# An attention, dense-MoE and routed-MoE kernel: register loads beside their branches, slot tables later, weight preparation and attention spread differently

## The chip, the cores and the metric

One core of one Trainium2 chip. The time is device microseconds of one execution; the kernel before took 888.47 us, the median of three runs (888.46 to 889.22). Lower is better. All durations below come from one profiled execution of the kernel before.

## The reference

Three stages, each feeding the next, on 4 batches of 576 tokens (2304 tokens, 512 features):

```python
# attention: 8 heads of 64; heads 0-3 with a local mask, heads 4-7 with a strided one (stride 32)
scores = where(mask, scale * q @ k.T, -1e9); attn = softmax(scores); x = attn @ v
# first MoE: LayerNorm and one dense feed-forward block for all tokens
xn = (x - mu) / sqrt(var + 1e-6) * g_ln
x = x + maximum(xn @ w_ch1, 0) @ w_ch2            # 512 -> 2048 -> 512
# second MoE: 8 experts, one for each token, 512 -> 1024 -> 512
e = argmax(logits)  where s == 0 or local_gate < 0.5, else the expert of the token before
out = softmax(logits)[e] * (maximum(x @ w1[e], 0) @ w2[e])
```

## The kernel before

TensorE (PE) computes every product with operands split into a high and a low part (three passes), so each weight has to be split before it is used. The program has one instruction stream for each engine; a planner written in Python puts the pieces of the stages into one another.

**First MoE with attention inside.** Tokens go in nine chunks `c` of 256. A step (c, f) is 24 matmuls: `mm1` (L628, matmuls at L635, result `ps_h`) for one block `f` of 16 of the hidden layer, ACT's ReLU (L637) and DVE's low part (L638), and `mm2` (L641, matmuls at L651, result `acc`). Chunks 0 and 1 run as pairs of interleaved steps, chunk 1 two steps behind (`LEAD`), because the weights are only arriving then; a step's number in that order is `t`. The dense weights come as 32 pieces `stg` by DMA, and each is split in a "weight turn": DVE L453, ACT L459 and L460 (`w_sign`), DVE L465, then the rounding to the high part at L479 (`w_split`, on ACT for all but the first four pieces) and POOL's subtraction L480 for the low part. `products` (L1050) decides before each step how many turns it issues: at least `need` (a turn for the weights that are read `WA` steps later), and otherwise `W_START + int(WR * t)`, with `W_START` 6 and `WR` 1.3 (L54, L1062, L1063). Attention of batch 0 stands ahead of the first chunk. That of batches 1, 2 and 3 is spread over spans of steps, `SPANS` (L51): the first from step 6 to step 24. It is made of units: transposes of q and k (L278), scores `ps_sc` (L317, L323), a softmax over DVE and ACT (`st`, `sm`: L335, L337, L350, L360 to L365), transposes of the probabilities (`ps_pt` L373, copied to `pt` at L381), and the product with v (`ps_o` L391, L409). The LayerNorm of chunk 1 (`ln_4`, variance matmuls at L571) stands between the first units.

**Routing and second MoE.** Tokens are listed by expert in tiles of 128. Four head tiles a0 to a3 of one expert, then the 14 sure tiles b0 to b13, whose expert is known only at run time, then leftovers in small slots; five slots s0, s1, s8, s9, s10 (`SURE`) always run, each behind the b-tile that `BEHIND` names (L67: 1, 3, 6, 9, 12). A tile is `e_mm1` (24 matmuls, L1396; the head tiles' at L1122), `h_prep` (transposes `ps_th` L1411, ACT L1412, DVE L1413 to `ht`), `e_mm2` (24 matmuls, L1424) and the weighted result `y` (L1427), scattered by POOL (L1428). For the head tiles the hidden layer's ReLU stands at L1126 (ACT) and its low part at L1127 (DVE). `x_prep` transposes the gathered tokens (`ps_tx` L878). A slot reads its weights unsplit from `raws`: L1358 (`s_mm1`) and L1384 (`s_mm2`).

Expert weights `raw` are split into `wx`, high at L778 (ACT) and low at L781 (DVE). Which tiles change the expert is known from a table `ti` only at run time, so each split and each load stands in a branch on a register: `flag` (L1306) loads one number of `ti` into a register of one engine, `resplit` (L1315) branches on it on ACT and on DVE, `next_load` (L1309) on SP, which issues the weight DMAs. In `run` (L1430) the first half of a tile's weights is split behind the product `e_mm1` of the tile before in the sequence, the second half behind `h_prep` of the tile itself, thus ahead of its `e_mm2`. In this run the expert changes at b4, b11 and b13. For slots, a table `ts` says if and for which expert (`used_s`, `load_small`). `small_places` (L1258) computes those tables, in a chain of small DVE instructions on one partition (`tb`, `vs`, `ts`; L1183 to L1188 and L1268 to L1279), then which tokens go to which slot (`chosen`: `ps_ve` L1227, `ps_ls` L1288 on PE). It is called just ahead of `e_mm2` of a2.

Of the kernel before, what the change touches and what calls it, by code (L numbers as in the profile page):

```python
# [18 lines left out]
ET = mybir.EngineType  # L19
# [5 lines left out]
NE, DF2 = 8, 1024  # L25
# [22 lines left out]
SMB, SM0, PT0, TL = 2, 4, 2, 1  # L48
WARM0, WARM, LB = 10, 5, 5
ORD = (((0, 1, 2), (0,)), ((3, 4, 5), (1,)), ((6, 7), (2,)))  # L50
SPANS = ((6, 24), (36, 54), (65, 86))  # L51

XB, LEAD = 5, 2
W_START, WR, WA, WI, W_DVE = 6, 1.3, 3, 5, 4  # L54
LN01, LN_AT, LN_W = (1, 1, 3, 1, 1, 4, 5, 9), (-7, -5, -4), (1, 2, 3, 4)
RT = ((0, 0, 1, 2, 3, 4, 6, 7, 8), (3, 4, 5, 6, 6, 7, 9, 10, 11))
RT_END = (0, 1, 2, 3, 4, 6, 8, 9, 10)
# [2 lines left out]
KA, NSURE = 4, 14  # L60
# [3 lines left out]
NLEAST = -(-(NT - NE * SMALL) // 128) - KA  # L64
NSM = 2 * NE
SURE = (0, 1, NE, NE + 1, NE + 2)
BEHIND = (1, 3, 6, 9, 12)  # L67
LAG1, LAG2 = 2, 4


# [1 line left out]
def attention_moe_moe(ctx: ExitStack, tc: tile.TileContext, q, k, v, g_ln, w_ch1, w_ch2, w_gate, w_local, w1, w2, out):  # L72
# [695 lines left out]
    def load_e(e, r, parts):  # L768

        if r < 2:  # L770
            src = w1[ds(e, 1)].rearrange("o d f -> (o d) f").rearrange("(i p) f -> p i f", p=128)[:, 2 * r:2 * r + 2]
        else:
            src = w2[ds(e, 1)].rearrange("o f d -> (o f) d").rearrange("(i p) o -> p i o", p=128)[:, 4 * (r - 2):4 * (r - 2) + 4]
        dst = parts[r]
        sp.dma_start(dst if r < 2 else dst.rearrange("p a (i o) -> p (a i) o", i=2), src)
# [479 lines left out]
    dve.tensor_copy(ti[:, 3, 0:NTILE], un)  # L1255


    def small_places():  # L1258

        vs = rt_p.tile([1, 2 * NSM], F32, tag="vs", name="vs").rearrange("p (a t) -> p a t", a=2)  # L1260
        dve.scalar_tensor_tensor(rem, cnt[:, 0, :], -128.0, cnt[:, 1, :], op0=ALU.mult, op1=ALU.add)
# [15 lines left out]
        dve.tensor_scalar(vs, vs, float(DM), None, op0=ALU.mult)  # L1277
        dve.tensor_tensor(over[:, 0:1], over[:, 0:1], over[:, 1:2], op=ALU.max)
        dve.tensor_tensor(ts[:, 2, 0:1], un[:, NSURE:NSURE + 1], over[:, 0:1], op=ALU.max)  # L1279
        sel, ix, er = chosen(vs, NSM, "_s")  # L1280
        for j in range(2):
            k = copies(NE * j)
            o = slice(NE * j, NE * j + NE)
# [19 lines left out]
    yp_ = [ps_acc.tile([128, 512], F32, tag=f"acc{i}", name=f"ps_y{i}") for i in range(2)]  # L1303
    turn = [0]

    def flag(i, n, engines):  # L1306
        return nc.values_load(ti[0:1, i, n:n + 1], engines=engines, min_val=0, max_val=NE - 1)

    def next_load(n, rs):  # L1309
        with tc.If(flag(1, n, [ET.SP]) > 0):  # L1310
            e = flag(2, n, [ET.SP])
            for r in rs:
                load_e(e, r, raw)

    def resplit(n, iis):  # L1315
        for eng, kinds, part in ((ET.Activation, ("InstActivation", "InstTensorCopy"), split_hi), (ET.DVE, ("InstTensorTensor",), split_lo)):
            last = next(i for i in reversed(nc.cur_bb.bb.instructions) if i.engine == eng and type(i).__name__ in kinds)
            v = flag(0, n, [eng])
            with tc.issue_after(last):
                with tc.If(v > 0):  # L1320
                    for j in iis:
                        part(j)
# [14 lines left out]
    pieces = {k: out.rearrange("t (h o) -> (t h) o", h=k) for k in (2, 4)}  # L1337

    def used_s(s, engines):
        return tc.If(nc.values_load(ts[0:1, 0, s[1]:s[1] + 1], engines=engines, min_val=0, max_val=1) > 0)  # L1340

    def set_of(i):
        return raw if i not in SURE and i % 2 == 0 else own

    def load_small(i):
        with used_s(("s", i), [ET.SP]):
            e = nc.values_load(ts[0:1, 1, i:i + 1], engines=[ET.SP], min_val=0, max_val=NE - 1)
            for r in range(4):
                load_e(e, r, set_of(i))

    def s_mm1(s):
        x, w, k = xs[s][0], set_of(s[1]), copies(s[1])
# [74 lines left out]
        act.activation(y, ps, AF.Copy, scale=pr)  # L1427
        pool.indirect_dma_start(out=out, out_offset=bass.IndirectOffsetOnAxis(ap=places(s)[1], axis=0), in_=y, in_offset=None, bounds_check=NT - 1, oob_is_err=False)  # L1428

    def run(seq, prev=None):  # L1430

        def weights(s, iis, rs):
            if s[0] == "b":
                resplit(s[1] + 1, iis)
                next_load(s[1] + 1, rs)

        for s in seq[:2]:
            if s not in xg:
                gather(s)
        if prev is None:  # L1440
            x_prep(seq[0])
            weights(seq[0], range(4), range(2))
        if len(seq) > 2:
            gather(seq[2])
        for i, s in enumerate(seq):
            e_mm1(s)
            if i + 1 < len(seq):
                x_prep(seq[i + 1])
                weights(seq[i + 1], range(4), range(2))
            p = seq[i - 1] if i else prev  # L1450
            if p:
                e_mm2(p)
                if p[0] == "s" and p[1] in SURE[:-1]:
                    load_small(SURE[SURE.index(p[1]) + 1])
            h_prep(s)
            weights(s, range(4, 8), range(2, 4))
            if i + 3 < len(seq):
                gather(seq[i + 3])
        e_mm2(seq[-1])

    for i in range(KA // 2):
        if i:
            e_mm1_two(i)
        for s in (("a", 2 * i + 2), ("a", 2 * i + 3)) if 2 * i + 2 < KA else (("b", 0),):
            if i:
                gather(s)
                x_prep(s)
        if 2 * i + 2 == KA:
            small_places()
            own += [new_blk([128, 2, 1024], F32, f"raws{r}") for r in range(4)]  # L1470
            load_small(0)
            resplit(1, range(4))
            next_load(1, range(2))
        for j in range(1 if 2 * i + 2 == KA else 2):
            e_mm2(("a", 2 * i + j))
    hp_ += [ps_m.tile([128, 512], F32, tag="m", name=f"ps_h2{i}") for i in range(2)]
    run([x for t in range(NSURE) for x in [("b", t)] + [("s", i) for i, b in zip(SURE, BEHIND) if b == t]], ("a", KA - 1))
    with tc.If(nc.values_load(ts[0:1, 2, 0:1], engines=mybir.ALL_ENGINES, min_val=0, max_val=1) > 0):  # L1478
        with tc.If(flag(3, NSURE, mybir.ALL_ENGINES) > 0):
            run([("b", t) for t in range(NSURE, NTILE)])  # L1480
# [38 lines left out]
```

## Time and profile before

| | |
|---|---|
| median of three runs | 888.47 us |
| the profiled execution's own time | 890.25 us |
| its span, first to last instruction | 888.5 us |
| mean granted TensorE clock | 0.985 |
| PE busy | 855.2 us (96%) |
| DVE, ACT, POOL busy | 469.9, 353.9, 148.5 us |

The profile shows one execution. An engine's busy time is the sum of its instructions; register loads, branches and DMA issues do not count in it. "Idle before" is the time for which an engine stood still ahead of an instruction, and the name behind the arrow is what ended that wait ("issue": nothing that the profile shows). PEclk is the TensorE clock that was granted, as a share of 2.4 GHz: 0.50 is 1.2 GHz.

### The profile page before, as it was taken

The page shows a single profiled execution, that of the slowest core. Times are in us where ns is not written, and L with a number is a line of the kernel's source. Part 1 is how long each engine was busy: PE and PEld are TensorE (multiplying, and loading weights), DVE is VectorE, ACT ScalarE, POOL GpSimd, SP SyncE. Part 2 cuts the span into 40 slices and gives each one's busy share as a digit, 9 for nine tenths or more (in the row PEclk, how much of TensorE's full clock was granted, in tenths as well). Part 3 has the DMA queues.
Part 4 walks back from the last instruction along what each step waited for, and adds up shares of the span by engine and source line. Part 5 has one row for each costly group of instructions (what it writes and reads, how often), then busy time and mean ns, then how long its engine had stood idle before and what let it go on. Part 6 is the DMA issues. An engine that isn't in the chain of part 4 may idle for free. (4 is left out here: it accounts for less than half of the span.)

```text
span 888.5 us, 18903 instructions
## 1 busy us (share of the span) xinstructions
PE 855.2 (96%) x7123; PEld 759.1 (85%) x7130; DVE 469.9 (53%) x1542; ACT 353.9 (40%) x857; POOL 148.5 (17%) x161
## 2 busy tenths in 40 slices
PE   9999898999999999999999999999989999999994
PEld 5678787899999999899999999999868777787873
DVE  4876676458656546666555554675731233211442
ACT  3687678542454233354211212332012244222543
POOL 2123233220120120120201212020221211210000
PEclk9999799999999999999999999999979999999998
DMA  9936245201212102210000000610446449440640
GB/s 182 261 112 207 55 130 144 56 8 52 65 41 45 49 13 61 49 26 18 23 1 25 1 25 2 214 49 26 166 157 225 149 147 391 153 144 27 242 165 16
DMA packets 96547, 87.17 MB, mean 98 GB/s; under 512 B 67378, under 2 KB 75574, under 8 KB 96440
## 3 DMA queue, kind: packets, MB, share of 16 engines
q1 hardware_dynamic: 89256, 69.61, 26.4%
q0 software_dynamic: 3552, 11.11, 3.8%
q10 hardware_dynamic: 3632, 5.09, 1.6%
q8 instruction: 59, 0.97, 0.4%
q14 instruction: 48, 0.39, 0.1%
HBM read 76.27 MB, written 9.97 MB: 97 GB/s over the span
## 5 line engine op out<-in xcount | busy, mean ns | idle before, releaser
L651 PE MATMUL acc<-h,w 128*128 128x256 f32 x1728 | 245.9, 290 | 2.4 <-DVE h L638 2.3
L635 PE MATMUL ps_h<-xc,w 128*128 128x256 f32 x1728 | 236.6, 286 | 0.1
L651 PEld LDWEIGHTS acc<-h,w 128*128 128x128 f32 x1728 | 218.8, 191 | 7.7 <-DVE h L638 3.6
L635 PEld LDWEIGHTS ps_h<-xc,w 128*128 128x128 f32 x1728 | 219.2, 192 | 2.1 <-DVE xc L619 0.5
L637 ACT ACTIVATE h<-ps_h 128x256 fp32r<-128x256 f32 x144 | 55.8, 388 | 221.4 <-PE ps_h L635 209.4
L638 DVE SCALAR_TENSOR_TENSOR h<-ps_h,h 128x256 fp32r<-128x256 f32 x144 | 60.5, 420 | 97.0 <-ACT h L637 96.7
L1396 PE MATMUL ps_h<-wx,xs 128*128 128x512 f32 x336 | 85.2, 409 | 0.0
L1424 PE MATMUL ps_y<-wx,ht 128*128 128x512 f32 x336 | 80.2, 394 | 2.0 <-ACT wx L778 1.7
L1396 PEld LDWEIGHTS ps_h<-wx,xs 128*128 128x128 f32 x336 | 64.3, 195 | 14.7
L1424 PEld LDWEIGHTS ps_y<-wx,ht 128*128 128x128 f32 x336 | 61.9, 188 | 15.2 <-ACT wx L778 2.3
L480 POOL TENSOR_TENSOR w<-stg,w 128x512 fp32r<-128x512 f32 x32 | 44.5, 1392 | 117.2 <-ACT w L479 75.6
L1427 ACT ACTIVATE y<-ps_y,pr 128x512 f32<-128x512 f32 x18 | 12.4, 687 | 84.5 <-PE ps_y L1424 56.7
L781 DVE TENSOR_TENSOR wx<-raw,wx 128x1024 fp32r<-128x1024 f32 x32 | 37.6, 1219 | 2.1 <-ACT wx L778 1.6
L1399 ACT ACTIVATE h<-ps_h 128x512 f32<-128x512 f32 x28 | 15.2, 595 | 58.8 <-PE ps_h L1396 58.8
L459 ACT ACTIVATE stg<-stg 128x512 f16<-128x512 f32 x27 | 37.1, 1375 | 0.2 <-DVE stg L453 0.2
L1413 DVE TENSOR_TENSOR ht<-ps_th,ht 128x512 fp32r<-128x512 f32 x28 | 18.1, 686 | 30.8 <-ACT ht L1412 27.4
L778 ACT CAST wx<-raw 128x1024 fp32r<-128x1024 f32 x32 | 31.9, 1055 | 6.4 <-PE acc L651 4.1
L892 DVE TENSOR_TENSOR xs<-ps_tx,xs 128x512 fp32r<-128x512 f32 x14 | 9.7, 691 | 46.3 <-ACTq L1320 35.3
L353 ACT ACTIVATE sm<-sm,st 128x54 f32<-128x54 f32 (+1 forms) x80 | 27.6, 347 | 13.3 <-DVE st L341 13.2
L1428 POOL DMA_INDIRECT out_dram<-y,idx x14 | 14.1, 1004 | 99.9 <-ACT y L1427 66.0
L894 DVE SCALAR_TENSOR_TENSOR pr<-io_e,e_rep,xg 128x8 f32<-128x8 f32 x14 | 3.1, 225 | 47.0 <-ACT y L1427 45.1
L1424 PE MATMUL ps_y<-wx,h2t 128*128 128x512 f32 x96 | 25.9, 414 | 1.5 <-DVE h2t L1127 1.3
(393 smaller groups left out, 1207.0 us busy)
## 6 DMA issues: line engine op xcount, KB each, us to landing
raws<-in_moe_w_dram SPq DMA_DIRECT2D x20, 1024.0 KB
stg<-in_moe_w_ch_dram SPq DMA_DIRECT2D x32, 512.0 KB
raw<-in_moe_w_dram SPq DMA_DIRECT2D x16, 1024.0 KB
xrows<-row ACTq DMA_DIRECT2D x9, 520.0 KB
qnat<-in_q_dram SPq DMA_DIRECT2D x48, 72.0 KB
knat<-in_k_dram SPq DMA_DIRECT2D x48, 72.0 KB
v<-in_v_dram SPq DMA_DIRECT2D x24, 72.0 KB
v<-in_v_dram SPq DMA_DIRECT2D x72, 18.0 KB
```

Of the source, the lines that this page charges most:

```text
L353: act.activation(sm[0:m, i, :], (ps if mode else sm)[0:m, i, :], AF.Exp, bias=st[0:m, 0, i:i + 1], scale=-1.0, **({} if mode else dict(acc ...
L459: keep(act.activation(t.bitcast(F16)[..., 1], f32(t[..., 1]), AF.Copy, scale=2.0 ** -112))
L480: keep(pool.tensor_tensor(w[:, 1], r, f32(w[:, 0]), op=ALU.subtract))
L635: pe.matmul(ps, w[:, a, d, o:o + 128], xcs[c][:, b_, d, :], start=(i == 0), stop=(i == 11))
L637: act.activation(h[:, 0, :], ps, AF.Relu)
L638: dve.scalar_tensor_tensor(h[:, 1, :], ps, 0.0, f32(h[:, 0, :]), op0=ALU.max, op1=ALU.subtract)
L651: pe.matmul(accs[c][d // 2][:, d % 2, :], w[:, a, f % 2, d * 128:(d + 1) * 128], h[:, b_, :], start=(f == 0 and (a, b_) == (0, 0) and d % ...
L778: act.copy(wx[i][:, 0, :], raw[i // 2][:, i % 2, :])
L781: dve.tensor_tensor(wx[i][:, 1, :], raw[i // 2][:, i % 2, :], f32(wx[i][:, 0, :]), op=ALU.subtract)
L1396: pe.matmul(hp_[fg], s_[:, a, d, :], wx[d][:, b_, 512 * fg:512 * fg + 512], start=(i == 0), stop=(i == 11))
L1413: dve.tensor_tensor(s_[1][:, 4 * g:4 * g + 4, :], ps, f32(s_[0][:, 4 * g:4 * g + 4, :]), op=ALU.subtract)
L1424: pe.matmul(ps, s_[a][:, f, :], wx[4 + f // 2][:, b_, 512 * (f % 2):512 * (f % 2) + 512], start=(i == 0), stop=(i == 23))
```

## The change

- The weight turns of the first MoE are issued at 1.0 a step instead of 1.3, and the first attention span goes from steps 6 to 24 to steps 8 to 26.
- `small_places` becomes two functions. The tables (`small_tables`) are computed in `run`, behind `e_mm1` of b0 and ahead of `e_mm2` of a3, and the places (`chosen` and what follows) behind `h_prep` of b0.
- A register's number is loaded once for each engine and kept (`loaded`), and its load stands just ahead of the branch that uses it, behind the last instruction that was put on that engine (`tc.issue_after`; `behind`).
- Slot s0 stands behind b2 instead of b1, and s1 behind b4 instead of b3.

```diff
--- before.py
+++ after.py
@@ -48,10 +48,10 @@
 SMB, SM0, PT0, TL = 2, 4, 2, 1
 WARM0, WARM, LB = 10, 5, 5
 ORD = (((0, 1, 2), (0,)), ((3, 4, 5), (1,)), ((6, 7), (2,)))
-SPANS = ((6, 24), (36, 54), (65, 86))
+SPANS = ((8, 26), (36, 54), (65, 86))
 
 XB, LEAD = 5, 2
-W_START, WR, WA, WI, W_DVE = 6, 1.3, 3, 5, 4
+W_START, WR, WA, WI, W_DVE = 6, 1.0, 3, 5, 4
 LN01, LN_AT, LN_W = (1, 1, 3, 1, 1, 4, 5, 9), (-7, -5, -4), (1, 2, 3, 4)
 RT = ((0, 0, 1, 2, 3, 4, 6, 7, 8), (3, 4, 5, 6, 6, 7, 9, 10, 11))
 RT_END = (0, 1, 2, 3, 4, 6, 8, 9, 10)
@@ -64,7 +64,7 @@
 NLEAST = -(-(NT - NE * SMALL) // 128) - KA
 NSM = 2 * NE
 SURE = (0, 1, NE, NE + 1, NE + 2)
-BEHIND = (1, 3, 6, 9, 12)
+BEHIND = (2, 4, 6, 9, 12)
 LAG1, LAG2 = 2, 4
 
 
@@ -1255,7 +1255,9 @@
     dve.tensor_copy(ti[:, 3, 0:NTILE], un)
 
 
-    def small_places():
+    tabs = []
+
+    def small_tables():
 
         vs = rt_p.tile([1, 2 * NSM], F32, tag="vs", name="vs").rearrange("p (a t) -> p a t", a=2)
         dve.scalar_tensor_tensor(rem, cnt[:, 0, :], -128.0, cnt[:, 1, :], op0=ALU.mult, op1=ALU.add)
@@ -1277,7 +1279,11 @@
         dve.tensor_scalar(vs, vs, float(DM), None, op0=ALU.mult)
         dve.tensor_tensor(over[:, 0:1], over[:, 0:1], over[:, 1:2], op=ALU.max)
         dve.tensor_tensor(ts[:, 2, 0:1], un[:, NSURE:NSURE + 1], over[:, 0:1], op=ALU.max)
-        sel, ix, er = chosen(vs, NSM, "_s")
+        tabs.append(vs)
+
+    def small_places():
+
+        sel, ix, er = chosen(tabs[0], NSM, "_s")
         for j in range(2):
             k = copies(NE * j)
             o = slice(NE * j, NE * j + NE)
@@ -1303,20 +1309,34 @@
     yp_ = [ps_acc.tile([128, 512], F32, tag=f"acc{i}", name=f"ps_y{i}") for i in range(2)]
     turn = [0]
 
+    regs = {}
+
+    def loaded(t, i, n, engines, top):
+        key = id(t), i, n, str(engines)
+        if key not in regs:
+            regs[key] = nc.values_load(t[0:1, i, n:n + 1], engines=engines, min_val=0, max_val=top)
+        return regs[key]
+
     def flag(i, n, engines):
-        return nc.values_load(ti[0:1, i, n:n + 1], engines=engines, min_val=0, max_val=NE - 1)
+        return loaded(ti, i, n, engines, NE - 1)
+
+    def behind(eng):
+
+        last = next((i for i in reversed(nc.cur_bb.bb.instructions) if i.engine == eng), None)
+        return tc.issue_after(last) if last is not None else ExitStack()
 
     def next_load(n, rs):
-        with tc.If(flag(1, n, [ET.SP]) > 0):
-            e = flag(2, n, [ET.SP])
-            for r in rs:
-                load_e(e, r, raw)
+        with behind(ET.SP):
+            v, e = flag(1, n, [ET.SP]), flag(2, n, [ET.SP])
+            with tc.If(v > 0):
+                for r in rs:
+                    load_e(e, r, raw)
 
     def resplit(n, iis):
         for eng, kinds, part in ((ET.Activation, ("InstActivation", "InstTensorCopy"), split_hi), (ET.DVE, ("InstTensorTensor",), split_lo)):
             last = next(i for i in reversed(nc.cur_bb.bb.instructions) if i.engine == eng and type(i).__name__ in kinds)
-            v = flag(0, n, [eng])
             with tc.issue_after(last):
+                v = flag(0, n, [eng])
                 with tc.If(v > 0):
                     for j in iis:
                         part(j)
@@ -1337,16 +1357,17 @@
     pieces = {k: out.rearrange("t (h o) -> (t h) o", h=k) for k in (2, 4)}
 
     def used_s(s, engines):
-        return tc.If(nc.values_load(ts[0:1, 0, s[1]:s[1] + 1], engines=engines, min_val=0, max_val=1) > 0)
+        return tc.If(loaded(ts, 0, s[1], engines, 1) > 0)
 
     def set_of(i):
         return raw if i not in SURE and i % 2 == 0 else own
 
     def load_small(i):
-        with used_s(("s", i), [ET.SP]):
-            e = nc.values_load(ts[0:1, 1, i:i + 1], engines=[ET.SP], min_val=0, max_val=NE - 1)
-            for r in range(4):
-                load_e(e, r, set_of(i))
+        with behind(ET.SP):
+            e = loaded(ts, 1, i, [ET.SP], NE - 1)
+            with used_s(("s", i), [ET.SP]):
+                for r in range(4):
+                    load_e(e, r, set_of(i))
 
     def s_mm1(s):
         x, w, k = xs[s][0], set_of(s[1]), copies(s[1])
@@ -1427,7 +1448,7 @@
         act.activation(y, ps, AF.Copy, scale=pr)
         pool.indirect_dma_start(out=out, out_offset=bass.IndirectOffsetOnAxis(ap=places(s)[1], axis=0), in_=y, in_offset=None, bounds_check=NT - 1, oob_is_err=False)
 
-    def run(seq, prev=None):
+    def run(seq, prev=None, tables=None, lists=None):
 
         def weights(s, iis, rs):
             if s[0] == "b":
@@ -1447,6 +1468,9 @@
             if i + 1 < len(seq):
                 x_prep(seq[i + 1])
                 weights(seq[i + 1], range(4), range(2))
+            if i == 0 and tables:
+                tables()
+                load_small(0)
             p = seq[i - 1] if i else prev
             if p:
                 e_mm2(p)
@@ -1454,6 +1478,8 @@
                     load_small(SURE[SURE.index(p[1]) + 1])
             h_prep(s)
             weights(s, range(4, 8), range(2, 4))
+            if i == 0 and lists:
+                lists()
             if i + 3 < len(seq):
                 gather(seq[i + 3])
         e_mm2(seq[-1])
@@ -1466,15 +1492,13 @@
                 gather(s)
                 x_prep(s)
         if 2 * i + 2 == KA:
-            small_places()
             own += [new_blk([128, 2, 1024], F32, f"raws{r}") for r in range(4)]
-            load_small(0)
             resplit(1, range(4))
             next_load(1, range(2))
         for j in range(1 if 2 * i + 2 == KA else 2):
             e_mm2(("a", 2 * i + j))
     hp_ += [ps_m.tile([128, 512], F32, tag="m", name=f"ps_h2{i}") for i in range(2)]
-    run([x for t in range(NSURE) for x in [("b", t)] + [("s", i) for i, b in zip(SURE, BEHIND) if b == t]], ("a", KA - 1))
+    run([x for t in range(NSURE) for x in [("b", t)] + [("s", i) for i, b in zip(SURE, BEHIND) if b == t]], ("a", KA - 1), small_tables, small_places)
     with tc.If(nc.values_load(ts[0:1, 2, 0:1], engines=mybir.ALL_ENGINES, min_val=0, max_val=1) > 0):
         with tc.If(flag(3, NSURE, mybir.ALL_ENGINES) > 0):
             run([("b", t) for t in range(NSURE, NTILE)])
```

The order of the instructions moves in places that the diff doesn't show. Numbers in tile names are buffers; lines of the changed kernel are 21 to 24 higher in this stretch. On **PE where attention of batch 1 begins** (`ps_tr` transposes, `ps_sc` scores, `ps_pt` transposes of the probabilities; `w_1_879` and so on are the weights of one turn):

```order
 L651 MATMUL acc_933<-h,w_1_879 128x256 x2
 L635 MATMUL ps_h<-xc,w_2_953 128x256 x12
-L278 MATMUL ps_tr<-iw,knat 128x96 x5
 L651 MATMUL acc_1074<-h,w_0_677 128x256 x6
 L651 MATMUL acc_1075<-h,w_0_677 128x256 x6
+L635 MATMUL ps_h<-xc,w_1_854 128x256 x12
+L651 MATMUL acc_932<-h,w_2_1040 128x256 x4
+L651 MATMUL acc_933<-h,w_2_1040 128x256 x4
+L651 MATMUL acc_932<-h,w_2_1040 128x256 x2
+L651 MATMUL acc_933<-h,w_2_1040 128x256 x2
+L635 MATMUL ps_h<-xc,w_2_953 128x256 x12
+L278 MATMUL ps_tr<-iw,knat 128x96 x5
```

The last transposes stand two steps later, and so does all that follows them. The variance matmuls L571, which stood behind the first `ps_pt` before, now stand ahead of it, behind the first scores.

On **ACT between the head tiles and b0** (`ti` is the routing table in SBUF, the `ISA` rows belong to the loads). Before, around the ReLU of the fourth head tile:

```order
L1307 TENSOR_LOAD ti
L1307 ISA x2
L1126 ACTIVATE h2t<-ps_h2t 128x512
L891 CAST xs<-ps_tx 128x512
L1320 COMPARE_AND_BRANCH
L778 CAST wx_7650<-raw_7649 128x1024
```

After the change:

```order
L1126 ACTIVATE h2t<-ps_h2t 128x512 x4
L891 CAST xs<-ps_tx 128x512
L1317 TENSOR_LOAD ti
L1340 COMPARE_AND_BRANCH
L778 CAST wx_7650<-raw_7649 128x1024
```

Before, five or six such loads stood between each two of the four ReLUs (L1126) and eight more behind the branch, 28 in all; now one load stands ahead of each tile's branch and none between the ReLUs. The same holds on DVE.

On **PE around slot s1** (`xss` and `raws` are the slot's tokens and weights, `wx` a b-tile's second weights, `ps_th` the transposes of a tile's hidden layer). Before, with s1 behind b3:

```order
L1411 MATMUL ps_th<-iw,h_9720 128x128 x8
L1340 TENSOR_LOAD ts
L1355 COMPARE_AND_BRANCH
L1358 MATMUL ps_h_9005<-raws_8893,xss 64x512 x4
L1358 MATMUL ps_h_9005<-raws_8894,xss 64x512 x4
L1355 UNCONDITIONAL_BRANCH x2
...
L878 MATMUL ps_tx<-iw,xg 128x128 x4
L1424 MATMUL ps_y_8630<-wx_7658,ht 128x512
```

After, with s1 behind b4:

```order
L1445 MATMUL ps_y_8630<-wx_7659,ht 128x512
L1317 TENSOR_LOAD ts
L1376 COMPARE_AND_BRANCH
L1379 MATMUL ps_h_8902<-raws_8815,xss 64x512 x4
L1379 MATMUL ps_h_8902<-raws_8816,xss 64x512 x4
L1376 UNCONDITIONAL_BRANCH x2
...
L1432 MATMUL ps_th<-iw,h_9743 128x128 x8
...
L1445 MATMUL ps_y_8631<-wx_7658,ht 128x512
```

The slot's first product now stands inside the second product of b3 instead of behind the transposes of a tile, so the transposes of b4's hidden layer and b4's second product follow each other with only the four transposes of tokens (`ps_tx`) between them. The same form is found at s8 and s9 after the change.

## Rows read from the trace of the kernel before

**Rows 1.** The page: busy time, its share of the span, instructions.

```profile
PE 855.2 (96%) x7123; PEld 759.1 (85%) x7130; DVE 469.9 (53%) x1542; ACT 353.9 (40%) x857; POOL 148.5 (17%) x161
```

**Rows 2.** Windows: length, busy us of each engine, PEclk, DMA share, GB/s.

```profile
60.00:75.00 15.00, 13.97 (x110) 12.98 (x110) 14.72 (x33) 13.24 (x22) 6.13 (x4) 1.00 0.41 121
75.00:205.00 130.00, 121.02 (x1132) 112.94 (x1133) 79.75 (x200) 84.59 (x159) 38.12 (x30) 0.96 0.32 90
```

**Rows 3.** The same view in windows of 5 us, and one of 46.

```profile
90.00:95.00 5.00, 2.75 (x25) 2.38 (x25) 4.90 (x14) 4.51 (x7) 2.34 (x2) 0.89 0.01 2
95.00:100.00 5.00, 4.16 (x20) 3.87 (x19) 2.31 (x6) 3.49 (x7) 1.55 (x2) 0.50 0.01 3
100.00:105.00 5.00, 5.00 (x28) 4.98 (x29) 3.34 (x18) 1.61 (x4) 0.00 (x0) 0.58 0.00 0
120.00:125.00 5.00, 3.42 (x44) 3.07 (x43) 4.39 (x12) 3.39 (x7) 1.68 (x2) 1.00 0.18 42
...
120.00:166.00 46.00, 40.96 (x446) 37.47 (x446) 31.15 (x79) 36.35 (x67) 15.73 (x12) 1.00 0.37 99
...
170.00:175.00 5.00, 5.00 (x50) 4.59 (x49) 0.51 (x2) 1.20 (x4) 0.00 (x0) 1.00 0.14 31
...
655.00:660.00 5.00, 4.24 (x15) 3.61 (x16) 1.57 (x14) 0.00 (x0) 0.62 (x1) 0.71 0.00 0
660.00:665.00 5.00, 5.00 (x15) 3.77 (x14) 1.25 (x9) 0.69 (x1) 2.40 (x3) 0.50 0.54 162
665.00:670.00 5.00, 5.00 (x21) 4.02 (x20) 0.46 (x4) 0.49 (x2) 0.00 (x0) 0.76 0.61 188
```

**Rows 4.** Timeline of PE: start, us, instruction, idle before and what ended it.

```profile
62.22 1.60 PE L635 MATMUL ps_h<-xc,w 128*128 128x256 f32 x12
...
65.10 2.23 PE L635 MATMUL ps_h<-xc,w 128*128 128x256 f32 x12
...
92.31 0.50 PE L373 MATMUL ps_pt<-iw,sm 128*96 128x128 f32 x3 [2.25 <-DVE sm L362]
...
96.32 1.86 PE L571 MATMUL ps_var<-mean_w,sq 128*128 128x1 f32 x8 [0.84 <-ACT pt L381]
```

**Rows 5.** Timeline of DVE ahead of that stall.

```profile
85.63 0.69 DVE L465 SCALAR_TENSOR_TENSOR stg<-stg 128x512 int32<-128x512 int32 x1 [2.71 <-ACT stg L460]
```

**Rows 6.** Timeline of ACT: one weight turn.

```profile
89.82 0.65 ACT L479 CAST w<-stg 128x512 fp32r<-128x512 f32 x1 [0.22 <-DVE stg L465]
90.38 1.34 ACT L459 ACTIVATE stg<-stg 128x512 f16<-128x512 f32 x1
91.75 0.69 ACT L460 ACTIVATE stg<-stg 128x512 f32<-128x512 f32 x1
...
93.21 0.67 ACT L479 CAST w<-stg 128x512 fp32r<-128x512 f32 x1 [0.46 <-DVE stg L465]
```

**Rows 7.** Timeline of PE where the second MoE begins.

```profile
651.22 1.67 PE L1424 MATMUL ps_y<-wx,h2t 128*128 128x512 f32 x6 [0.20 <-DVE tb L1183]
654.16 0.50 PE L1424 MATMUL ps_y<-wx,h2t 128*128 128x512 f32 x1 [1.27 <-DVE h2t L1127]
655.76 0.40 PE L1227 MATMUL ps_ve<-vs,mean_w 1*128 1x32 f32 x2 [1.10 <-DVE vs L1277]
```

**Rows 8.** Timeline of ACT there.

```profile
646.87 0.60 ACT L1126 ACTIVATE h2t<-ps_h2t 128x512 fp32r<-128x512 f32 x1 [2.27 <-issue]
650.33 0.60 ACT L1126 ACTIVATE h2t<-ps_h2t 128x512 fp32r<-128x512 f32 x1 [2.86 <-issue]
```

**Rows 9.** Timeline of PE: b13's second product, behind its split.

```profile
872.47 2.86 PE L1424 MATMUL ps_y<-wx,ht 128*128 128x512 f32 x11 [1.67 <-ACT wx L778]
```

**Rows 10.** Timeline of PE: an ordinary tile's token transposes.

```profile
748.20 0.60 PE L878 MATMUL ps_tx<-iw,xg 128*128 128x128 f32 x4
```

**Rows 11.** Timelines of ACT and DVE: b13's hidden layer.

```profile
870.40 1.07 ACT L1412 CAST ht<-ps_th 128x512 fp32r<-128x512 f32 x2
...
871.01 1.29 DVE L1413 TENSOR_TENSOR ht<-ps_th,ht 128x512 fp32r<-128x512 f32 x2 [9.03 <-ACT ht L1412]
```

## The prediction

> **What bounds the kernel now.** I read the busy times first: PE works for 855.2 of 888.5 us, every other engine for at most 53% [rows 1]. So only two things can be won: PE's idle time, some 33 us of it, and time in which PE works at a lower clock. Windows over the span then show where both lie. Apart from the start and the tail, which the change doesn't touch, there are two places: the steps in which the dense weights are split and attention of batch 1 begins (75 to 170 us), and the begin of the second MoE (645 to 667 us). Of the 145 us from 60 to 205, PE works for 13.97 + 121.02 = 134.99 [rows 2], so 10.0 us are idle. The windows of 5 us give the granted clock [rows 3]: 0.89, 0.50 and 0.58 from 90 to 105, and 0.71, 0.50 and 0.76 from 655 to 670. Half speed (0.50) is 1.2 GHz, the rest of these windows ran at 2.4. What each lost: 5 x (0.11 + 0.50 + 0.42) = 5.15 us at the first place and 5 x (0.29 + 0.50 + 0.24) = 5.15 us at the second. Both follow a hole in PE's work, which the timelines name.
>
> **The first MoE.** The hole at 90 us is a wait of 2.25 us for the first unit's probabilities (DVE L362), then 0.84 us for their copy [rows 4]. DVE was late because of the weights: it stood 2.71 us still in front of a piece that ACT had not finished (L465 behind L460), with the unit's small reductions queued behind it in order [rows 5]. ACT is what is scarce: a turn costs it 1.34 + 0.69 + 0.67 = 2.70 us, and with the wait for DVE between them L479 follows L479 by 93.21 - 89.82 = 3.39 us [rows 6]. The step without attention takes PE 65.10 - 62.22 = 2.88 us [rows 4]. At 1.3 turns a step (3.5 us of ACT) ACT cannot keep up with plain steps, and the work of a unit comes on top.
>
> What the change does there, against the profiled execution:
> - The first unit begins two steps later. DVE, which worked 14.72 of 15 us before 75 [rows 2], gets its softmax off its back for that time, and the variance matmuls now stand ahead of the first `ps_pt`, so that PE has 1.86 us [rows 4] of other work there. The waits of 2.25 and 0.84 don't vanish: the chain of DVE through the unit is as long, and the LayerNorm's small operations are threaded into it. I take 1.5 of the 3.09 as left: -1.6 (bounds 0 and -3.1).
> - From 120 to 166 us PE works for 40.96 of 46 [rows 3]: 5.0 us of smaller waits, mostly for ACT's copies. With 1.0 instead of 1.3 turns a step ACT has 0.3 x 2.70 = 0.8 us more a step. I let half of them go: -2.5 (bounds 0 and -5).
> - The half-speed stretch. It began behind 2.25 us of idle (PE 2.75 of 5 from 90); behind 1.58 us of idle from 120 (3.42 of 5) the clock stayed at 1.00 [rows 3]. An idle of 1.5 is nearest to the second row, so I let the stretch go: -5.15 (bounds 0 and -5.15).
> - New: steps 6 and 7 have a turn and no attention, so that ACT's 3.39 stands against PE's 2.88: +0.5 each, +1.0 (bounds 0 and 2).
> - New: the last of the 38 weight turns is issued at t = 28 instead of 25, near the products that read it. ACT did nothing to speak of from 170 to 175 (1.20 of 5 busy) [rows 3] and can take work there, so the cover is that room; should a turn come late, its 2.70 us of ACT bounds the cost: +1.0 (bounds 0 and 2.7).
>
> Sum: -1.6 - 2.5 - 5.15 + 1.0 + 1.0 = **-7.25**.
>
> **The second MoE's begin.** `e_mm2` of a2 is held up three times: 0.20 by a table, 1.27 by the low part of its hidden layer (DVE L1127), 1.10 by `vs`, the last number of the slot table [rows 7]. The low part is late because ACT's ReLUs are: 2.27 and 2.86 us of "issue" idle stand ahead of the third and fourth [rows 8], and it is there that five and six register loads stand in ACT's order. That makes 2.27 / 5 = 0.45 and 2.86 / 6 = 0.48 us a load.
>
> The Trainium skill ("Runtime: NRT & Kernel Launch", section "Instruction fetch mechanics") gives about 0.2 us a register for such a load, from HBM; by it these eleven would be 2.2 of the 5.13 us, and the wait that goes would be about 1.1 instead of 2.3 us below. The row decides here, since nothing else stands between these ReLUs.
>
> With the loads gone from between them, the ReLUs come when their products do, and `vs` is no longer wanted by PE before the transposes of b0. The tables' small DVE instructions still stand between the first L1127s in the new order, so not all goes: of 0.20 + 1.27 + 1.10 = 2.57 I leave 0.3, -2.3 (bounds 0 and -2.57). The hole ahead of the second half-speed stretch was these waits; with them goes the stretch, -5.15 (bounds 0 and -5.15). `ps_ve` and `ps_ls` are moved, not removed. One load remains ahead of each branch, at 0.45 us on ACT and DVE, which wait for PE there: nothing; if that cover were gone it would be 0.45 a tile on 14 tiles, 6.3.
>
> New costs come from the slots. b4 changes its expert, and the second half of its weights is split behind its `h_prep`. Before, the whole of b5's first product covered that. Now s1 stands there, its product has been moved further up, and `e_mm2` of b4 follows at once. That is b13's case, which waits 1.67 us [rows 9]; the token transposes of 0.60 [rows 10] stand between here: +1.1 (bounds 0 and 1.7). At s8 and s9, likewise hoisted, a tile's `ht` is wanted 0.6 us behind its transposes, but needs a copy and a low part of half of 1.07 and half of 1.29 [rows 11], 1.2 us: +0.6 each, +1.2 (bounds 0 and 2.4). Loads of slot weights for s8 start later by the move of s1 but are wanted behind two more tiles' work: nothing.
>
> Sum: -2.3 - 5.15 + 1.1 + 1.2 = **-5.15**.
>
> Both: -12.4 us. The profiled execution took 890.25, so 877.85 by it; that execution is 1.8 above the median of 888.47, and against the median I say **876.1 us**.
>
> **Rivals.**
> 1. *One of the half-speed stretches stays or comes at a new place.* For it: one row in which the clock stayed doesn't make a rule, and my 1.5 us of idle is an estimate. Against: that row [rows 3]. 876.1 + 5.15 = 881.2.
> 2. *Both stay,* as the small DVE instructions still stand in the way at the second MoE, and the first unit is as late as before: 876.1 + 10.3 = 886.4, with the waits half there 887. This is also the case in which the change doesn't do what it says. The tables' instructions are still between the L1127s in the order, which speaks for it; the loads are surely gone from there, which speaks against.
> 3. *Slower: late weights.* The last twelve turns, pushed back, each come to ACT in the step that reads them, and PE waits one pass of 1.34 us [rows 6] each: 12 x 1.34 = 16.1 in place of the 1.0 taken, and such waits bring a half-speed stretch with them, +5.15: 876.1 + 15.1 + 5.15 = 896.4. It decides from about 0.7 us a turn (8 + 5 us against 12.4). Against it: ACT's room from 170 to 175 [rows 3], and `need`, which still asks for a turn ahead of its reader. For it: DVE, POOL and ACT take a turn in series, so a late start isn't caught up.
>
> The Trainium skill ("TensorE: Matmul & The Clock Gate", Part 1) says that the gate keeps a beat of its own, not started by the kernel, so that the place at which a kernel's clock changes varies from run to run. The three runs lie within 0.76 us of each other while one stretch costs 5.15, so the trace gives it little support here. As a rival of its own it would make single runs of 881 beside 876, and it shares rival 1's chance.
>
> **How the numbers follow.** Forecast 0.50; rival 1 0.27; rival 2 0.11; rival 3 0.07; the rest, 0.05, is smaller new waits that add up to no change. The lower bounds of all terms give: stage one -3.1 - 5 - 5.15 = -13.3, second -2.57 - 5.15 = -7.7, together -21, so 867.5; all of them at once is not likely, and 869 is the low end. The high end takes in both rivals 1 and most of 2: 886.5. About 1.8 us (0.2%) is what a measurement of this kernel can tell from no change, so below 886.7 is faster and above 890.2 slower. The forecast, rival 1 and most of rival 2 are faster: 0.83; part of rival 2 and the rest no change: 0.09; rival 3 and a little: 0.08.
>
> **What would show it.** In the profile after: granted clock 1.00 in all windows from 80 to 110 and from 645 to 665; L1126 back to back with PE's products, `e_mm2` of a2 in about 6 us instead of 11; the wait ahead of the first `ps_pt` at most 1.5; a wait for ACT's L778 at b4's second product of about 1.1. I am wrong if the clock falls at the first attention unit again, if PE waits for L465, L479 or L480 near t = 28, or if L1127 still ends PE's waits in a2.

## The result and the profile after

| | before | changed |
|---|---|---|
| median | 888.61 us (4 runs, 888.46 to 889.22) | 895.18 us (4 runs, 894.30 to 895.28) |
| ratio, 95% interval | | 1.007 (1.0053 to 1.0088) |
| profiled execution, its span | 890.25, 888.5 us | 895.25, 893.5 us |
| mean granted clock | 0.985 | 0.990 |

The change is 0.7% slower where 1.4% faster was forecast, and outside the range. Yet the two places that the prediction was about look as it said. Windows of the changed kernel, columns as in [rows 2]:

```profile
75.00:205.00 130.00, 120.85 (x1152) 111.65 (x1153) 82.05 (x213) 84.76 (x160) 37.64 (x30) 1.00 0.31 91
90.00:95.00 5.00, 4.70 (x43) 4.37 (x44) 2.29 (x7) 4.43 (x6) 2.11 (x2) 1.00 0.90 312
95.00:100.00 5.00, 3.54 (x36) 3.22 (x32) 4.58 (x15) 4.40 (x8) 1.83 (x2) 1.00 0.09 31
100.00:105.00 5.00, 4.71 (x43) 4.09 (x43) 4.93 (x15) 3.35 (x6) 1.32 (x1) 1.00 0.00 0
...
640.00:660.00 20.00, 19.74 (x110) 16.81 (x110) 5.56 (x25) 3.93 (x7) 6.02 (x6) 1.00 0.85 294
...
720.00:725.00 5.00, 0.00 (x0) 0.00 (x0) 0.00 (x0) 0.00 (x0) 0.00 (x0) 0.67 1.02 367
725.00:730.00 5.00, 1.82 (x6) 0.67 (x8) 0.39 (x2) 0.00 (x0) 0.00 (x0) 0.50 1.03 401
...
720.00:740.00 20.00, 11.33 (x47) 6.54 (x47) 1.28 (x5) 2.31 (x5) 0.75 (x1) 0.74 0.68 255
```

Both half-speed stretches of [rows 3] are gone in this execution (other executions with the same first MoE lose some clock there, see below), and PE's waits at the beginning of the second MoE have shrunk to 0.26 us. What is new stands from 720 to 740: no engine works for 5 us, while the DMA engines are full. The timeline of PE names the wait, at the first product of slot s1 (`SPq` is the queue of DMAs that SP issues; the first line is the same product in the kernel before, the others are the changed kernel):

```profile
721.93 3.65 PE L1358 MATMUL ps_h<-raws,xss 128*64 128x512 f32 x16
...
717.97 0.60 PE L878 MATMUL ps_tx<-iw,xgs 128*128 128x128 f32 x4
718.33 1.41 PE L1445 MATMUL ps_y<-wx,ht 128*128 128x512 f32 x5
728.18 5.48 PE L1379 MATMUL ps_h<-raws,xss 128*64 128x512 f32 x16 [8.45 <-SPq L1331]
733.59 4.61 PE L1445 MATMUL ps_y<-wx,ht 128*128 128x512 f32 x19
738.04 1.03 PE L1432 MATMUL ps_th<-iw,h 128*128 128x128 f32 x8
738.91 0.60 PE L878 MATMUL ps_tx<-iw,xg 128*128 128x128 f32 x4
```

The timeline of SP's DMA queue tells when the weights were asked for. Its first line is the kernel before, where s1's were the second four of eight, thus issued by 710; then the changed kernel, and DVE's split that frees the buffers of `raw`:

```profile
665.96 43.79 SPq L775 DMA_DIRECT2D raws<-in_moe_w_dram  x8
...
650.21 13.28 SPq L775 DMA_DIRECT2D raws<-in_moe_w_dram  x4
714.72 2.64 SPq L775 DMA_DIRECT2D raw<-in_moe_w_dram  x2
718.88 2.47 SPq L775 DMA_DIRECT2D raws<-in_moe_w_dram  x4
...
712.22 4.63 DVE L781 TENSOR_TENSOR wx<-raw,wx 128x1024 fp32r<-128x1024 f32 x4 [0.25 <-ACT wx L778]
```

The 4 MB for s1 (`raws`) were issued at 718.88, right behind the 2 MB of the next expert (`raw`), while PE asked for them at 719.7. The 8.45 us of wait and the product at 5.48 instead of 3.65 us (in the kernel before, at full clock) are 10.3 us. The clock in the two windows is 0.67 and 0.50.

### The profile page after: what moved, and what is told of

The parts are those of the page before. It is cut to its first block, busy times and chain, and to the rows that moved or that the text cites. A ratio compares the mean times of both kernels' runs of the same rounds, so it can differ in the third digit from the quotient of the medians.

```text
span 893.5 us, 18761 instructions
## 1 busy us (share of the span) xinstructions
PE 852.6 (95%) x7123; PEld 752.1 (84%) x7130; DVE 469.6 (53%) x1542; ACT 353.9 (40%) x857; POOL 148.1 (17%) x161
## 5 line engine op out<-in xcount | busy, mean ns | idle before, releaser
L651 PE MATMUL acc<-h,w 128*128 128x256 f32 x1728 | 245.2, 289 | 3.4 <-DVE h L638 1.9
L651 PEld LDWEIGHTS acc<-h,w 128*128 128x128 f32 x1728 | 217.9, 190 | 9.6 <-DVE h L638 3.6
L638 DVE SCALAR_TENSOR_TENSOR h<-ps_h,h 128x256 fp32r<-128x256 f32 x144 | 60.5, 420 | 98.8 <-ACT h L637 98.2
L1417 PE MATMUL ps_h<-wx,xs 128*128 128x512 f32 x336 | 83.4, 401 | 0.8 <-ACT wx L778 0.8
L1417 PEld LDWEIGHTS ps_h<-wx,xs 128*128 128x128 f32 x336 | 61.6, 188 | 17.0 <-ACT wx L778 1.4
L781 DVE TENSOR_TENSOR wx<-raw,wx 128x1024 fp32r<-128x1024 f32 x32 | 37.5, 1220 | 2.2 <-ACT wx L778 1.8
L465 DVE SCALAR_TENSOR_TENSOR stg<-stg 128x512 int32<-128x512 int32 x27 | 18.6, 689 | 13.0 <-ACT stg L460 12.5
```

Of the source, the lines that this page charges most:

```text
L465: keep(dve.scalar_tensor_tensor(t[..., 1], t[..., 1], 3, t[..., 0], op0=ALU.logical_shift_left, op1=ALU.bitwise_or))
L638: dve.scalar_tensor_tensor(h[:, 1, :], ps, 0.0, f32(h[:, 0, :]), op0=ALU.max, op1=ALU.subtract)
L651: pe.matmul(accs[c][d // 2][:, d % 2, :], w[:, a, f % 2, d * 128:(d + 1) * 128], h[:, b_, :], start=(f == 0 and (a, b_) == (0, 0) and d % ...
L781: dve.tensor_tensor(wx[i][:, 1, :], raw[i // 2][:, i % 2, :], f32(wx[i][:, 0, :]), op=ALU.subtract)
L1417: pe.matmul(hp_[fg], s_[:, a, d, :], wx[d][:, b_, 512 * fg:512 * fg + 512], start=(i == 0), stop=(i == 11))
```

## The experiments

**Is it the queue, the slot's place, or the loads?** Three variants of the changed kernel, then the slots' move alone in the kernel before.

*Slots back* (s0's gather moved behind its places, so that it can stand behind b1):

```diff
-BEHIND = (2, 4, 6, 9, 12)
+BEHIND = (1, 3, 6, 9, 12)
...
-        if len(seq) > 2:
+        if len(seq) > 2 and not (lists and seq[2][0] == "s"):
             gather(seq[2])
...
                 lists()
+                if seq[2][0] == "s":
+                    gather(seq[2])
```

> The changed kernel with BEHIND as before (s0 behind b1, s1 behind b3); s0's gather is put behind its places, all else as changed. Theory Q (in the changed kernel the load of s1's weights is queued on SP behind the load of expert weights that waits for b4's split): with s0 back, s1's load is issued some 10 us ahead of that one, so the 8.45 us wait, the half-speed time behind it (some 4 to 5 us) and the two waits for L778 (0.76 and 1.42) go: 879 to 882 us. Rival H (s1's first product is too early for its weights because it was moved into the product before): still a wait of several us ahead of L1379 at s1, 890 or more. Rival R (the register loads' new places or the later tables cost the time): as changed, 894 to 896.

Measured: 883.32 us (10 runs, 882.96 to 884.73); against the kernel before 0.9949 (0.9930 to 0.9967). The wait is gone. So the rest of the change doesn't cost anything in sum, and rival R is out.

*Slot's load ahead of the expert's* on SP:

```diff
-                weights(seq[i + 1], range(4), range(2))
+                weights(seq[i + 1], range(4), range(2), False)
...
                     load_small(SURE[SURE.index(p[1]) + 1])
+            if i + 1 < len(seq) and seq[i + 1][0] == "b":
+                next_load(seq[i + 1][1] + 1, range(2))
             h_prep(s)
```

> The changed kernel, slots where the change has them; only SP's order differs: the load of a tile's next expert weights is issued behind that of the next slot's weights instead of ahead of it. Theory Q: s1's load is issued some 10 us earlier (at about 707 instead of 719), the 8.45 us wait shrinks to under 1 and the clock stays up; the wait of 1.42 us for b4's split stays: 881 to 884 us. Rival H: 4 MB from 707 on are not there at 720 either, a wait of 2 us or more stays, 885 to 890. Rival R: 894 to 896.

Measured: 884.72 us (884.22 to 885.29). Its SP queue and PE:

```profile
648.28 58.28 SPq L775 DMA_DIRECT2D raws<-in_moe_w_dram  x8
715.26 20.99 SPq L775 DMA_DIRECT2D raw<-in_moe_w_dram  x4
```

```profile
718.86 1.40 PE L1445 MATMUL ps_y<-wx,ht 128*128 128x512 f32 x5
720.19 3.65 PE L1379 MATMUL ps_h<-raws,xss 128*64 128x512 f32 x16
723.78 4.63 PE L1445 MATMUL ps_y<-wx,ht 128*128 128x512 f32 x19
728.24 1.04 PE L1432 MATMUL ps_th<-iw,h 128*128 128x128 f32 x8
729.12 0.60 PE L878 MATMUL ps_tx<-iw,xg 128*128 128x128 f32 x4
731.14 5.81 PE L1445 MATMUL ps_y<-wx,ht 128*128 128x512 f32 x24 [1.42 <-ACT wx L778]
```

With the slots where the change has them and all else equal, s1's load is out by 706.6 and its product waits for nothing. The 1.42 us for b4's split stay. The queue's order is a necessary part of the loss, and rival H, in which the product is too early whatever the queue does, is out.

*Only s0 back:*

```diff
-BEHIND = (2, 4, 6, 9, 12)
+BEHIND = (1, 4, 6, 9, 12)
```

> The changed kernel with s0 back behind b1 and s1 left behind b4. Theory Q: it is s0's place that sets when s1's load is issued, so the 8.45 us wait goes although s1 hasn't moved, and only the uncovered split of b4 (1.42 us at its second product) stays: 880 to 883 us. Rival P (it is s1's own place behind b4, where the expert changes): 892 to 896.

Measured: 884.81 us (nine of ten runs 884.07 to 885.51, one 890.72). No wait at s1, although it stands behind b4; b4's second product waits 1.37 for its split. So it was s0's place that made s1's load late: `load_small` of the next slot is called behind the second product of the slot before, and s0 behind b2 puts that call behind `next_load` of b4.

*The slots' move alone,* in the kernel before (`BEHIND = (2, 4, 6, 9, 12)`, nothing else):

> The kernel before with only the slots moved (s0 behind b2, s1 behind b4); loads, tables and the first MoE as before. Theory Q: the place of s0 alone puts the load of s1's weights behind the load that waits for b4's split; PE waits some 8 us at s1's first product and loses 4 to 5 us more to the clock: slower than before by 10 to 14 us, 898 to 902. Rival R (the new places of register loads on SP hold up that load): as before or 1 to 2 us slower, 888 to 890.

Measured: 887.94 us (884.14 to 891.80), ratio 0.9986 (0.9964 to 1.0008): no loss that can be told, and theory Q as I had put it fails. The load is as late as in the changed kernel; the timelines of SP and PE:

```profile
719.57 2.65 SPq L775 DMA_DIRECT2D raw<-in_moe_w_dram  x2
723.32 3.50 SPq L775 DMA_DIRECT2D raws<-in_moe_w_dram  x4
```

```profile
725.60 5.74 PE L1424 MATMUL ps_y<-wx,ht 128*128 128x512 f32 x24
731.17 1.03 PE L1411 MATMUL ps_th<-iw,h 128*128 128x128 f32 x8
732.92 1.94 PE L1358 MATMUL ps_h<-raws,xss 128*64 128x512 f32 x8 [0.71 <-ACT ht L1412]
735.38 1.94 PE L1358 MATMUL ps_h<-raws,xss 128*64 128x512 f32 x8 [0.52 <-SPq L1310]
```

but the product stands behind the transposes, and PE asks for the weights at 732.2, not at the fifth matmul of the product before. It waits 0.71 us for their first half (put down to ACT's `ht`, which this product doesn't read) and 0.52 for the second. The other half of the loss is the product's place on PE. Two more runs settle that.

*Product held in place,* the changed kernel otherwise:

```diff
-        with used_s(s, [ET.PE]):
+        with behind(ET.PE), used_s(s, [ET.PE]):
```

> The changed kernel, slots and SP's order as changed; only the slot's first product on PE is held behind what stands ahead of it in the program (the transposes of the tile before), as it stood in the kernel before, instead of five matmuls into the second product. Theory I (the loss needs two things together: the load of s1's weights behind the one that waits for b4's split, and s1's product some 9 us earlier on PE): the load is issued at about 719 as in the changed kernel, but PE asks for it only at about 724 to 729 and the wait ahead of L1379 falls from 8.45 to between 0 and 4; the half-speed time behind it goes in most runs; the waits of 0.5 us at s8 and s9 go too: 883 to 888 us. Rival Q alone (a late load costs the same wherever its reader stands): the wait stays near 8, 893 or more.

Measured: 883.63 us (883.03 to 885.95), ratio 0.9963 (0.9941 to 0.9985). SP and PE:

```profile
715.83 2.65 SPq L775 DMA_DIRECT2D raw<-in_moe_w_dram  x2
720.00 2.97 SPq L775 DMA_DIRECT2D raws<-in_moe_w_dram  x4
```

```profile
725.03 1.03 PE L1432 MATMUL ps_th<-iw,h 128*128 128x128 f32 x8
728.82 5.47 PE L1379 MATMUL ps_h<-raws,xss 128*64 128x512 f32 x16 [2.76 <-SPq L1331]
```

The load is as late, the wait 2.76 instead of 8.45, within what theory I gave. This profile is of the slowest of ten runs (885.95): the clock falls behind the wait (0.67 from 730 to 735), and the product takes 5.47 us. Together with the run before: a late load alone costs 1.2 to 2.8 us of wait, an early product alone (slot's load first) nothing, both 8.45.

*What moved the product up?* The register loads alone, in the kernel before:

```diff
+            with tc.issue_after(last):
+                v = flag(0, n, [eng])
...
+        return tc.If(loaded(ts, 0, s[1], engines, 1) > 0)
```

(and `loaded`, `behind`, `next_load` and `load_small` as in the change).

> The kernel before with only the register loads changed (each number once, just ahead of its branch); tables, slots and the first MoE as before. If the loads between the ReLUs are what held ACT, the idle of 2.27 and 2.86 us ahead of the third and fourth L1126 goes, and with it PE's wait of 1.27 for L1127; the wait for vs (1.10) stays: 1 to 2 us faster than before in runs of the same clock. If it was something else, both idles stay and the time is as before.

Measured: 888.66 us (886.82 to 893.31), ratio 1.0013 (0.9988 to 1.0038). In its order of instructions the product of s1 already stands behind the fifth matmul of L1440:

```profile
710.13 1.41 PE L1440 MATMUL ps_y<-wx,ht 128*128 128x512 f32 x5
711.47 3.65 PE L1374 MATMUL ps_h<-raws,xss 128*64 128x512 f32 x16
```

So the hoist comes with the new register loads, not with the slots; whether because they are kept or because they stand elsewhere wasn't separated. And the gain at the head tiles is there, for ACT:

```profile
645.15 0.60 ACT L1126 ACTIVATE h2t<-ps_h2t 128x512 fp32r<-128x512 f32 x1 [3.22 <-PE ps_h2t L1122]
646.84 0.60 ACT L1126 ACTIVATE h2t<-ps_h2t 128x512 fp32r<-128x512 f32 x1 [1.09 <-PE ps_h2t L1122]
```

The ReLUs wait for PE now, no longer for "issue" as in [rows 8]. PE still waits 1.66 us ahead of `ps_ve`, and the hoisted products cost it 0.52, 0.47, 0.18, 0.47 and 0.18 elsewhere, and the clock still falls at the second MoE's begin (0.71 from 650 to 655): in sum no gain.

**What is the first MoE's part worth?** Alone in the kernel before (`SPANS` and `WR` as changed):

> The kernel before with only the first MoE's part of the change (the span from step 8 to 26, 1.0 turns a step). By the changed kernel's trace (597.15 against 599.54 us at the same instruction of the last chunk) it is worth 2.4 us: 886 to 886.5 us. By the prediction's term, 7.25: 881 us. If the second MoE's half-speed stretch depends on when it is reached, 881 or 891.

Measured: 886.41 us (883.35 to 887.74); the kernel before beside it took 888.22, but from 882.99 to 890.38 in 31 runs. Its 0.9993 (0.9971 to 1.0015) can't be told from no change. The other way round, the slots-back kernel with the first MoE as before (`SPANS` 6 to 24, `WR` 1.3):

> The first experiment's kernel (all of the change but the slots) with the first MoE as before. Theory K (the two half-speed stretches come in some runs and not in others, and the change of the first MoE makes the first one rarer): runs spread from 881 to 886, half-speed behind the first unit of attention in some, none at the begin of the second MoE. By the prediction's terms (7.25 for the first MoE): 890.5. By the trace (2.4): 885.7.

Measured: 885.89 us (884.87 to 886.58), 2.6 more than the 883.32 with it. But the two were run in different sets, and each against the kernel before of its own set they can't be told apart: 0.9961 (0.9948 to 0.9975) and 0.9949 (0.9930 to 0.9967). The clock falls in the profiles of both, less in the slots-back kernel's (first line) than in this one's:

```profile
80.00:100.00 20.00, 19.90 (x162) 18.63 (x160) 11.29 (x30) 16.72 (x24) 7.94 (x6) 0.91 0.45 142
...
80.00:100.00 20.00, 17.08 (x131) 15.38 (x130) 11.88 (x30) 16.14 (x24) 7.70 (x6) 0.82 0.34 116
100.00:120.00 20.00, 19.49 (x183) 17.92 (x182) 14.62 (x42) 14.45 (x26) 5.25 (x4) 0.92 0.54 150
```

Then the span alone, with 1.3 turns a step:

> The first experiment's kernel with the turns back at 1.3 a step and the attention span left at 8 to 26. If the later start of attention is what keeps the first half-speed stretch away: no such stretch, and the waits for late weights from 182 to 192 us (0.17, 0.64, 0.46 and what lies around them) go: 882 to 883.5 us. If the rate is what does it: a stretch in most runs, 885 to 887.

Measured: 885.24 us (883.61 to 888.33), against the kernel before of its set 0.9987 (0.9966 to 1.0008). The late weights at 182 to 192 us are on time again, but in the profile the clock falls at another place (0.91 from 120 to 140) and the runs spread more. So these runs give neither the span nor the rate a worth of its own; the rate alone wasn't tried.

**How firm are the half-speed stretches?** The kernel before once more:

> The kernel before once more, unchanged, for a second profile. Theory K: one or both half-speed stretches may be missing, with the same waits ahead of them; 883 to 890 us.

Measured: 883.11 us. Its windows and its PE:

```profile
90.00:95.00 5.00, 2.91 (x21) 2.49 (x22) 4.90 (x13) 4.53 (x7) 2.57 (x2) 0.76 0.01 2
95.00:100.00 5.00, 5.00 (x37) 4.71 (x36) 3.86 (x10) 3.32 (x6) 1.34 (x2) 0.84 0.01 3
100.00:105.00 5.00, 5.00 (x36) 4.98 (x35) 3.39 (x17) 3.15 (x7) 0.51 (x1) 0.72 0.19 44
...
650.00:655.00 5.00, 2.63 (x11) 1.64 (x10) 2.57 (x13) 0.00 (x0) 0.00 (x0) 1.00 0.03 11
655.00:660.00 5.00, 5.00 (x25) 4.06 (x25) 2.16 (x18) 0.69 (x1) 3.02 (x3) 1.00 0.35 85
660.00:665.00 5.00, 5.00 (x26) 4.07 (x25) 0.59 (x4) 1.57 (x3) 1.04 (x1) 1.00 0.22 83
```

```profile
651.61 0.51 PE L1424 MATMUL ps_y<-wx,h2t 128*128 128x512 f32 x1 [1.28 <-DVE h2t L1127]
653.20 0.40 PE L1227 MATMUL ps_ve<-vs,mean_w 1*128 1x32 f32 x2 [1.09 <-DVE vs L1277]
```

The last two waits are those of [rows 7], to 0.01 us, and the clock stays at 1.00 behind them. The same program with the same idle loses its clock in one execution and not in the next.

So one pair of profiles can't price a stretch, but all the profiles together can. Take the moment at which PE reaches one instruction of the last chunk (the L651 that waits some 0.7 us for DVE's L638). The five profiles with the first MoE as before have it at 597.12 (this one) to 599.54 (the first), 598.4 in the mean; the eight with the span and the rate as changed at 597.04 to 598.21, 597.4 in the mean. So the first MoE's part is worth about 1 us. In five of those eight the clock falls between 90 and 105 all the same, by 1.7 us each, counted as window length times missing clock; in the slots-back kernel's profile that costs nothing: PE is 0.42 us behind the changed kernel's at 75 us (75.81 and 75.39) and 0.40 at 166 us (166.96 and 166.56), as it waits less for the first unit. From that instruction to the first product of b1 it takes 72.0 to 76.7 us in the four profiles with tables and loads as before, 74.7 in the mean, and 67.0 to 67.3 in all nine with both as changed. The clock falls there in three of the four, and in none of the nine.

**A version that beats both.** First the slots-back kernel with the products held in place and s10 behind b13, to cover the last split:

```diff
-BEHIND = (1, 3, 6, 9, 12)
+BEHIND = (1, 3, 6, 9, 13)
...
-        with used_s(s, [ET.PE]):
+        with behind(ET.PE), used_s(s, [ET.PE]):
```

> The first experiment's kernel with the slot's first product held in its place as in the run before, and the last slot s10 behind b13 instead of b12, so that its product stands between the last split and b13's second product. The waits of 1.67 (b13) and of 0.47, 0.29, 0.47 and 0.18 us (s8 and s9) go: 883.3 - 3.1 = 880.2 us, 880 to 881.5. If the end of the program is set by the last scatter, and s10's second product and scatter come last instead, up to 1 us of it is given back.

Measured: 886.44 us (885.72 to 888.35): worse by 3. The 1.67 us at b13 went, but in the profile s10's hidden layer waits behind ACT's four casts, and the last scatter (POOL) 4.53 us for the one before it to land, so the end is set by a new chain:

```profile
861.98 0.69 PE L1390 MATMUL ps_th<-iw,h2s 128*128 128x128 f32 x2 [3.56 <-ACT h2s L1381]
```

```profile
875.74 0.98 POOL L1408 DMA_INDIRECT out_dram<-y,idx_s  x1 [4.53 <-DMA out_dram<-y,idx]
```

So without the last slot's move:

> The first experiment's kernel (slots as before) with the slot's first product held in its place on PE, the last slot left behind b12. The waits of 0.47, 0.29, 0.47 and 0.18 us at s8 and s9 go, as they went in the two kernels before it that hold the product: 883.3 - 1.4 = 881.9 us, 881.5 to 882.5. If the covers are the same in sum and PE only waits elsewhere: 883 to 883.6.

Measured: **880.14 us** (6 runs, 879.85 to 880.88), ratio to the kernel before 0.9929 (0.9906 to 0.9953), and 3.2 below the slots-back kernel (of another set) where 1.4 were expected. The four waits at s8 and s9 are gone, and so is one of 0.52 us at b4's second product. What else of the 3.2 it is wasn't separated; a second product that is cut in two takes 1.41 + 4.61 = 6.02 us instead of the 5.72 of one in one piece, as busy time that no wait shows.

## Why the prediction was wrong

**The step that failed** is the one sentence "Loads of slot weights for s8 start later by the move of s1 but are wanted behind two more tiles' work: nothing." It costed the move of the slots by s8's load and left out s1's. Moving s0 moves the call that loads s1's weights, past `next_load` of b4, on a queue whose next entry waits until b4's first weights are split (DVE L781, 712.22 to 716.85). With the product of s1 moved up on PE, which the order in the section on the change shows and the prediction used only to cost b4's cover, load and reader met: 8.45 us of wait and 1.8 us of slow product. At the transposes of b5's hidden layer the changed kernel stands at 757.06 us against 754.11 before, +2.95; at the first product of b1 it had stood at 664.12 against 676.25, -12.1. In between lie 15.1 us: these 10.3, the two waits for b4's split (0.76 and 1.42), 1.2 of `ps_ls` matmuls that now stand behind that product's begin, and the rest busy time, most of it of three products cut in two at some 0.3 each.

Point by point:
- *Waits of the first MoE, -1.6 and -2.5.* Wrong. From 75 to 205 PE works 120.85 of 130 us, 121.02 before [rows 2]: the idle went from 8.98 to 9.15 us. The wait for L362 is 1.74 instead of 2.25 (at most 1.5 was forecast), and others took the place of the rest (1.35 and 1.36 us ahead of `ps_tr`).
- *The half-speed stretch there, -5.15.* It is gone in this profile, but at the last chunk the changed kernel is only 2.4 us ahead (the same instruction at 597.15 against 599.54), and the kernel before's second profile is there at 597.12: the 2.4 us come of a late first profile, and by the mean of all profiles the whole part is worth about 1 us, where 7.25 were forecast. In five of eight profiles the clock still falls near the first unit, which the prediction named as a sign of being wrong. Window length times missing clock charges too much: it counts slow time that a wait behind it makes good, and also for PE's 3.09 idle us within; by busy time it is 2.75 x 0.11 + 4.16 x 0.50 + 5.00 x 0.42 = 4.5. Late weights (1.27, below) are in the 1 us; what else is wasn't separated.
- *New costs there, +1.0 and +1.0.* Three waits for late weights at 182 to 192 us, 0.17 + 0.64 + 0.46 = 1.27: right for the second. At steps 6 and 7 no new wait: the first was nothing.
- *The second MoE's begin, -2.3 and -5.15.* Right in the changed kernel's profile: 2.57 us of waits became 0.26, the clock 1.00; of the 12.1 us at b1, 9.7 arise here, 1.2 of them the `ps_ls` matmuls. But the first profile had the worst of it: the stretch comes and goes in the kernel before. By the mean of all profiles 7.5 arise here (74.7 and 67.1), 6.3 without `ps_ls`, against the forecast of 7.45: the mechanism holds, the size is about right, the 5.15 of one execution was too much.
- *b4's split, +1.1.* Measured 1.42 at b4's second product, and 0.76 at its first, which the term left out: 2.2 in sum, above its bound of 1.7. *s8 and s9, +0.6 each:* 0.52 + 0.18 and 0.47 + 0.18. *One load a branch, nothing:* so it was. The terms for s8, s9 and the loads were good; the missed term was larger than all of them.
- *Rival 3* had the right sign and the wrong place: weights that come late, but those of a slot. *Rival 1* came true in part, as a consequence: a stretch at a new place, behind that wait.
- *The rule on the clock's beat* (the Trainium skill, "TensorE: Matmul & The Clock Gate", Part 1) has the place of a clock change vary from run to run, and I set it aside as three runs lay within 0.76 us. The trace agrees with it: the kernel before's two profiles have 0.89, 0.50, 0.58 and 0.76, 0.84, 0.72 in the same windows from 90, and its 31 runs lie 7.4 us apart, those with a mean clock of 0.985 at 889.24 to 890.38, those from 0.990 on at 882.99 to 885.98. My three runs were too few.
- *The rule of 0.2 us a register load* (the Trainium skill, "Runtime: NRT & Kernel Launch", section "Instruction fetch mechanics"): with the eleven loads gone both "issue" waits, 5.13 us, are gone, and waits for PE stand in their place; in the kernel before's second profile the two idles are 2.27 and 2.86 us again. The profile of the kernel before has the 28 loads of ACT line by line (ns, lowest, median and highest):

```profile
L1307 ACTq TENSOR_LOAD <-ti x28: 272/277/473, 636.0 to 655.5; - x28
L1307 ACTq FUSED_REGOPS  x28: 147/147/162, 636.5 to 655.8; - x28
L1307 ACTq SEQ_ASSERT  x28: 18/18/29, 636.7 to 656.0; - x28
```

With the two steps behind it a load from SBUF takes 0.277 + 0.147 + 0.018 = 0.44 us, so the row decided rightly; the load alone, 0.28, is nearer to the 0.2.

## What to carry to other kernels

A load that is issued "behind the work that frees its buffer" is in fact issued behind all that its queue holds by then: when a step moves in the program, list for each queue what it has been moved past and what that entry waits for. Two moves that are free alone can meet, a load that goes later and its reader that goes earlier, so cost them as a pair. And before a clock stretch is put on the bill, look whether it is in every execution: here the kernel's own spread, 7.4 us, was as large as the gain.

## What the runs showed of the hardware

- Behind the same two waits (1.28 and 1.09 us, 1.27 and 1.10) PE's clock stayed at 2.4 GHz in one execution and fell to 1.2 in another.
- With both loads under way the DMA moved 367 and 401 GB/s in the two windows from 720 to 730, its engines full; s1's 4 MB, issued within 2.47 us, let PE start 9.3 us after the first was issued.
